# One linear-attention and GeGLU kernel: phi in another form on three engines, K weights on ScalarE's DMA queue, later weights behind the crossbar transposes

## The chip, the cores and the metric

The kernel runs on one core of a Trainium2 chip. The metric is the device time of one execution in microseconds (us), as the median of several runs.

## The reference

The input x has 2048 rows of 576 values in bf16. After a layer norm, two branches read the same normalised rows, and both results are added to x. Branch A is linear attention with 32 heads of 18 values; branch B is a gated feed-forward network (FFN) with 4608 hidden values. Cut to what matters:

```python
xn = _layernorm(x)
# branch A
qkv = (xn @ wqkv).reshape(B, S, 3, H, Dh)         # H = 32, Dh = 18
phi = lambda t: jnp.where(t > 0, t + 1, jnp.exp(t)) + 1e-6
pq, pk = phi(q), phi(k)
kv  = jnp.einsum("bhsd,bhse->bhde", pk, v)
z   = jnp.einsum("bhsd->bhd", pk)
num = jnp.einsum("bhqd,bhde->bhqe", pq, kv)
den = jnp.einsum("bhqd,bhd->bhq", pq, z)[..., None] + 1e-6
attn = (num / den) @ wo
# branch B
ffn = (gelu(xn @ w_gate) * (xn @ w_up)) @ w_down
out = x + attn + ffn
```

## The kernel before, in words

The 2048 rows are 16 tiles of 128 rows. Work falls into two large stages, and each engine executes its own instructions strictly in the order in which the program issues them.

**The attention stage.** For every tile n the kernel does these steps; the names are those of the code.

- `ln_stats` (L212, L213) on VectorE (DVE) takes mean and variance, `ln_rstd` (L217, L218) on ScalarE (ACT) takes the reciprocal root, `ln_norm` (L221) on DVE writes the normalised rows `xn`, and `ln_dup` (L227) copies the last 64 columns once more, on GpSimd (POOL) for the first four tiles and on DVE after that.
- `xn` is transposed into `xnT`. The first four tiles go through TensorE (PE), `transposes` (L236), and a copy out of PSUM, `tp_copy` (L239). The other twelve go through the DMA crossbar, `dma_transposes` (L242), issued from SyncE (SP).
- `k_half` (L250) computes K for one tile in two halves of 288 columns, into PSUM banks 5 and 6 (for tile 1 into banks 0 and 1).
- phi of K is made in three steps a half: `k_relu` (L270) and `k_exp` (L274) on ACT make exp(-relu(-t)) in the f32 tile `phi_e`, and `k_sum` (L278) on DVE adds max(t, 0) from PSUM and writes `pk`. The name `hT` in the profile at L278 is the storage that `pk` shares.
- `g_accumulate` (L294) adds pk of the tile, multiplied with `xn`, to the matrix G, from which the kv product and z are later made without ever forming V. `pk` has one more column of ones, from which the constant 1e-6 of phi is added when G is copied out (`g_copy`, L539 to L546).

The Q side works in 20 units (`q_unit`, L347), each a group of up to seven heads by 512 rows. phi of Q takes `q_relu` (L381) and `q_exp` (L385) on ACT, `q_eps` (L389) on POOL, which adds 1e-6, and `q_sum` (L393) on DVE. The first 14 units run singly; the last six run as three pairs (`q_pair`) whose two matmul streams use the two halves of the PE rows (L318).

The order of all this is written out by hand. The tables `STEPS` and `Q_STEPS` give each step a due time per tile, the last entry repeating every `TILE` = 2.94; the list `todo` is sorted by those times and issued in that order. Some small matmuls without use (`spin`, L138) keep PE busy early on. In `todo` also stand the loads of the V weights (`load_w(2, ...)`, L109 and L112) and of the first four FFN weight blocks (`load_gu`, L176 to L180), one step a tile from 18.0 on. They are issued by SP, between the crossbar transposes.

At the start SP issues all loads in one queue: x tiles 0, 1, 2 and 3, then the K weights, x tiles 4 to 7, the Q weights, and x tiles 8 to 15. ACT loads its function table (L132) meanwhile.

**The FFN stage.** For four groups of 512 rows, 18 blocks (`gu_pair`) each compute two chunks of gate and up values. A `_Unit` runs the gate and the up matmuls side by side on the two halves of the PE rows, in two passes `p1` and `p2`; between the passes the halves change banks, and a `nop` on another engine (the relay, L327) orders that turn. The relay engine is SP for blocks 0 and 1 and POOL for later ones. `load_gu` for a later block stands ahead of `p1` on SP from block 1 on, and waits until its buffers are free. Then ACT takes the gelu (L634), DVE multiplies (L635), and after 18 blocks the down projection (L664, L669) follows.

Of the kernel before, what the change touches and what calls it, by code (L numbers as in the profile page):

```python
# [8 lines left out]
ACT = mybir.ActivationFunctionType  # L9
ALU = mybir.AluOpType  # L10
# [5 lines left out]
P = 128  # L16
HP = 64
# [21 lines left out]
NWARM = 38  # L39
TD = 4  # L40
XW = 642
PKW = 578


class _Ring:
# [11 lines left out]
def kernel(  # L57
# [34 lines left out]
    def load_x(n0, cnt):  # L92
        nc.sync.dma_start(x_sb[:, n0:n0 + cnt, :], x_view[:, n0:n0 + cnt, :])  # L93
# [10 lines left out]

    wq_lo = apool.tile([P, D], BF16, name="wq_lo")

    def load_w(which, k0=0, k1=4):
        c = slice(which * D, (which + 1) * D)
        nc.sync.dma_start(  # L109
            wqkv_sb[:, k0:k1, c], A_wqkv[k0 * P:k1 * P, c].rearrange("(kt p) c -> p kt c", p=P))  # L110
        if k1 == 4:
            nc.sync.dma_start(wqkv_sb[0:HP, 4, c], A_wqkv[512:576, c])  # L112
            if which == 0:
                nc.sync.dma_start(wq_lo[HP:P, :], A_wqkv[512:576, c])

# [11 lines left out]
    make_identity(nc, ident[:])  # L127
    eps_ln = const.tile([P, 1], F32, name="eps_ln")
    nc.vector.memset(eps_ln[:], EPS_LN)
    eps_att = const.tile([P, 1], F32, name="eps_att")  # L130
    nc.vector.memset(eps_att[:], EPS_ATT)
    nc.scalar.preload_act_table_set("natural_log_exp_and_others")  # L132
    nc.vector.memset(wqkv_sb[HP:P, 4, :], 0.0)

    def spin(count):
# [47 lines left out]

    xn = apool.tile([P, NS, XW], BF16, name="xn")
    nc.gpsimd.memset(xn[:, :, 640:641], 1.0)
    nc.gpsimd.memset(pk[:, :, D:D + 1], 1.0)

    bmask = const.tile([P, CR], F32, name="bmask")
    bm3 = bmask[:].rearrange("p (h e) -> p h e", e=DH)
# [75 lines left out]
        hs = slice(hf * HALF, (hf + 1) * HALF)  # L265
        return ps_all[:, k_bank(n, hf), :HALF], k_e[n][:, hs], pk[:, n, hs]

    def k_relu(n, hf):
        ps, e, _ = k_part(n, hf)
        nc.scalar.activation(out=e, in_=ps, func=ACT.Relu, scale=-1.0)  # L270

    def k_exp(n, hf):
        _, e, _ = k_part(n, hf)
        nc.scalar.activation(out=e, in_=e, func=ACT.Exp, scale=-1.0)  # L274

    def k_sum(n, hf):
        ps, e, out_ = k_part(n, hf)
        nc.vector.scalar_tensor_tensor(out=out_, in0=ps, scalar=0.0, in1=e, op0=ALU.max, op1=ALU.add)  # L278

    G_A = {
        0: [(0, 0, 0, 288), (1, 0, 288, 289)],
        1: [(2, 0, 0, 288), (3, 0, 288, 289)],
        4: [(0, 288, 0, 224), (1, 289, 224, 223), (2, 288, 447, 130)],
    }
    G_B = {2: [(5, 0, 0, 288), (6, 0, 288, 289)], 3: [(0, 0, 0, 288), (1, 0, 288, 289)]}
    eps_sum = const.tile([P, KT], F32, name="eps_sum")

    def g_accumulate(n, pieces):  # L290
        for kt, ps_ in pieces.items():
# [80 lines left out]
    def q_at(i):  # L372
        sc, c = divmod(i, NCH)
        rows = DH * HCH[c]
        if i not in q_e:
            q_e[i] = phi_tile()[:rows, :SC]
        return q_e[i], q_out[i], pqT[:rows, c, sc * SC:(sc + 1) * SC]

    def q_relu(i):
        e, ps, _ = q_at(i)  # L380
        nc.scalar.activation(out=e, in_=ps, func=ACT.Relu, scale=-1.0)  # L381

    def q_exp(i):
        e, _, _ = q_at(i)
        nc.scalar.activation(out=e, in_=e, func=ACT.Exp, scale=-1.0)  # L385

    def q_eps(i):
        e, _, _ = q_at(i)
        nc.gpsimd.tensor_scalar(out=e, in0=e, scalar1=1.0, scalar2=EPS_ATT, op0=ALU.mult, op1=ALU.add)  # L389

    def q_sum(i):
        e, ps, out_ = q_at(i)
        nc.vector.scalar_tensor_tensor(out=out_, in0=ps, scalar=0.0, in1=e, op0=ALU.max, op1=ALU.add)  # L393

    def mask_pair(dst, b4, b1):

# [63 lines left out]
    def den_norm(sc, c, q, pieces):  # L460
# [14 lines left out]
    TILE = 2.94  # L475
    x_ = None
    STEPS = [
        (ln_stats, [3.05, 3.99, 6.43, 7.37, 8.65, 10.92, 14.71, 16.48]),
        (ln_rstd, [4.17, 5.11, 7.56, 8.55, 10.38, 13.51, 15.94, 18.79]),
        (ln_norm, [x_, 5.70, 8.31, 9.59, 11.86, 14.13, 17.42, 20.27]),  # L480
        (ln_dup, [5.61, 6.18, 8.79, 10.07, 12.34, 14.61, 17.90, 20.75]),
        (transposes, [x_, 6.58, 9.09, 10.37]),
        (tp_copy, [x_, 7.00, 9.54, 11.09]),
        (dma_transposes, [x_, x_, x_, x_, 12.58, 14.85, 18.14, 20.99]),
        (lambda n: k_half(n, 0), [6.87, 9.38, 10.66, 13.72, 16.57, 20.24, 22.61, 25.46]),
        (lambda n: k_half(n, 1), [7.48, 8.10, 11.27, 14.33, 17.18, 19.63, 22.00, 24.85]),
        (lambda n: k_relu(n, 0), [7.99, 10.81, 11.93, 14.46, 17.31, 21.11, 23.35, 26.20]),
        (lambda n: k_relu(n, 1), [8.27, 9.26, 12.67, 15.20, 18.05, 20.37, 22.78, 25.59]),
        (lambda n: k_exp(n, 0), [8.98, 12.95, 12.39, 14.92, 17.77, 21.57, 23.91, 26.76]),
        (lambda n: k_exp(n, 1), [10.10, 11.65, 13.23, 15.66, 18.51, 20.83, 23.63, 26.48]),  # L490
        (lambda n: k_sum(n, 0), [9.93, 13.41, 12.85, 15.65, 18.60, 22.03, 24.45, 27.30]),
        (lambda n: k_sum(n, 1), [10.56, 12.44, 13.77, 16.12, 18.97, 21.29, 24.09, 26.94]),
        (lambda n: g_accumulate(n, G_A), [12.97, 14.94, 15.82, 17.80, 23.22, 24.10, 26.08, 29.13]),
    ]

    Q_STEPS = [
        (q_unit, [11.89, 18.55, 20.85, 26.83, 29.88]),
        (q_relu, [13.94, 19.76, 22.28, 28.04, 31.09]),
        (q_exp, [16.37, 24.19, 27.04, 30.10, 33.16]),
        (q_eps, [17.05, 24.87, 27.72, 30.78, 33.84]),  # L500
        (q_sum, [18.00, 25.75, 28.60, 31.66, 34.72]),
    ]
    NQ = 12

# [6 lines left out]

    todo = [*timed(STEPS, NS), *timed(Q_STEPS, NQ)]

    for n, (na, nb, ta, tb, ca, cb) in enumerate([(4.93, 5.31, 5.31, 5.91, 5.62, 6.16)]):
        todo += [
            (na, lambda n: ln_norm(n, 0, 3 * P), n), (nb, lambda n: ln_norm(n, 3 * P, D), n),
            (ta, lambda n: transposes(n, 0, 3, 7), n), (tb, lambda n: transposes(n, 3, KT, 4), n),
            (ca, lambda n: tp_copy(n, 0, 3, 7, acopy), n), (cb, lambda n: tp_copy(n, 3, KT, 4, vcopy), n),
        ]

    todo += [(t, spin, count) for t, count in [(5.70, 4), (6.23, 3), (6.60, 5), (10.42, 2)]]

    loads = [lambda n, i=i: load_gu(i // 2, i % 2) for i in range(2 * NWBUF)]
    loads.insert(1, lambda n: load_w(2, 0, 2))
    loads.insert(3, lambda n: load_w(2, 2, 4))
    todo += [(18.0 + TILE * i, step, 0) for i, step in enumerate(loads)]
    todo.sort(key=lambda x: x[0])

    tail = next(i for i, (_, step, n) in enumerate(todo) if step is STEPS[-1][0] and n == NS - 1) + 1
# [2 lines left out]


    def g_copy(kt, pieces, on):

        m = P if kt < 4 else HP + 1
        eps = eps_sum[:m, kt:kt + 1]
        b, col, _, w = pieces[kt][-1]
        nc.vector.tensor_scalar_mul(out=eps, in0=ps_all[:m, b, col + w - 1:col + w], scalar1=EPS_ATT)  # L539
        for (b, col, d0, w), eng in zip(pieces[kt][::-1], on):  # L540
            w = min(w, D - d0)
            out_, in_ = g_sb[:m, kt, d0:d0 + w], ps_all[:m, b, col:col + w]
            if eng is nc.scalar:
                nc.scalar.activation(out=out_, in_=in_, func=ACT.Identity, bias=eps, scale=1.0)
            else:
                nc.vector.tensor_scalar_add(out=out_, in0=in_, scalar1=eps)  # L546

    for n in range(NS):
        g_accumulate(n, {2: G_B[2]})
    g_copy(4, G_A, (nc.vector, nc.scalar, nc.vector))  # L550
    g_copy(0, G_A, (nc.scalar, nc.vector))
    g_copy(1, G_A, (nc.scalar, nc.vector))
    for _, step, n in todo[tail:]:
        step(n)
    q_unit(12)
    for step in (q_relu, q_exp, q_eps, q_sum):
        step(12)
    for n in range(NS):
# [43 lines left out]
    def gu_pair(sc, k):  # L602
# [4 lines left out]
        for i in range(GUB):  # L607
            b = [banks.next(), banks.next()]
            fcol = slice(i * P, (i + 1) * P)

            def lhs(a, rows, kt, fcol=fcol):
                if kt == 4:
                    return wr[rows, fcol]
                return (wg, wu)[a][rows, kt, fcol]

            u = _Unit([ps_all[:, b[0], :], ps_all[:, b[1], :]], lhs, lambda a, rows, kt: xnT[rows, kt, cs],
                      nc.sync if blk < 2 else nc.gpsimd)
            if blk > 0:
                load_gu(blk + NWBUF - 1, i)
            u.p1()  # L620
            units.append((b, u))
# [106 lines left out]
```

## Time and profile before

| what | value |
|---|---|
| median of 3 runs | 525.21 us (524.9 to 526.15) |
| profiled execution | 526.45 us |
| its span, first to last instruction | 524.7 us |
| PE busy | 517.2 us (99%) |
| DVE busy | 248.4 us (47%) |
| ACT busy | 147.9 us (28%) |
| POOL busy | 40.1 us (8%) |
| mean granted TensorE clock | 1.000 |

The profile is one execution on the chip. PE is TensorE's matmuls, PEld its weight loads, SPq the issuing of SyncE. Times in it count from the span's start. A busy PE is not PE at its peak: matmuls are pipelined and their ends are modelled, so the durations of neighbours overlap. An engine's idle time is put down to what released it.

### The profile page before, as it was taken

Reading aid. Unit: us, or ns where it says so; the run is one execution under the profiler, and the core shown is the slowest. Engines: PE = TensorE matmul, PEld = TensorE weight load, DVE = VectorE, ACT = ScalarE, POOL = GpSimd, SP = SyncE. Lnnn points to the kernel's source line nnn. Section 1 sums busy time; section 2 is a strip of 40 time slices with the busy share of each in tenths; the row PEclk is TensorE's granted clock in tenths of the full one; section 3 lists DMA queues with packets and bytes.
Section 4 is the critical chain, followed back from the end, with each engine's and each line's share of the span. In section 5 each row is a group of like instructions: output and inputs, shape, how many; then the busy total and the mean of one; then the engine's idle time right before and its main releaser. Section 6 shows DMA issues by size and latency. Waiting matters only on the chain.

```text
span 524.7 us, 10664 instructions
## 1 busy us (share of the span) xinstructions
PE 517.2 (99%) x4502; PEld 315.8 (60%) x4502; DVE 248.4 (47%) x426; ACT 147.9 (28%) x301; POOL 40.1 (8%) x63
## 2 busy tenths in 40 slices
PE   7999999999999999999999999999999999999997
PEld 7767764555577754444577744444777544445775
DVE  7887545977348423333388134333584233333110
ACT  5989563233230012332200033232000123222000
POOL 2012130121001100000011000000011000000000
PEclk9999999999999999999999999999999999999999
DMA  8565009999500035555300065555100355540000
GB/s 262 135 156 119 1 2 240 264 268 265 169 21 24 12 103 158 158 144 158 108 12 13 28 174 143 156 159 151 32 22 12 104 158 157 144 130 1 12 11 24
DMA packets 106443, 57.90 MB, mean 110 GB/s; under 512 B 13402, under 2 KB 105754, under 8 KB 106394
## 3 DMA queue, kind: packets, MB, share of 16 engines
q1 hardware_dynamic: 106394, 57.21, 38.8%
q8 instruction: 35, 0.57, 0.4%
q14 instruction: 14, 0.11, 0.1%
HBM read 52.86 MB, written 2.36 MB: 105 GB/s over the span
## 4 chain that ended last, share of the span: by engine, by line
PE 96%; DMA 2%; ACT 1%; DVE 0%; SPq 0%; issue 0%; DVEq 0%
PE ps_all L318 55%; PE ps_all L664 27%; PE ps_all L669 4%; PE ps_all L294 3%; PE ps_all L250 3%; PE ps_all L347 3%; DMA wqkv_sb<-in_A_wqkv_dram 1%; DMA xnT<-xn 1%; PE ps_all L442 1%; PE ps_all L424 0%; PE ps_all L646 0%; SPq L93 0%; ACT phi_e L270 0%; DVE hT L278 0%; ACT xnT L239 0%; ACT phi_e L274 0%
## 5 line engine op out<-in xcount | busy, mean ns | idle before, releaser
L318 PE MATMUL ps_all<-xnT,wg 64*128 64x512 bf16 x1152 | 273.0, 376 | 0.0
L318 PE MATMUL ps_all<-xnT,wu 64*128 64x512 bf16 x1152 | 271.6, 376 | 0.0
L635 DVE TENSOR_TENSOR hT<-ps_all,gl 128x512 bf16<-128x512 f32 x144 | 99.4, 691 | 161.2 <-ACT gl L634 160.7
L634 ACT ACTIVATE gl<-ps_all 128x512 f32<-128x512 f32 x144 | 86.0, 598 | 312.7 <-PE ps_all L318 295.8
L318 PEld LDWEIGHTS <-wu 64*128 64x128 bf16 x1152 | 108.1, 94 | 66.0 <-SPq L327 0.7
L318 PEld LDWEIGHTS <-wg 64*128 64x128 bf16 x1152 | 108.1, 94 | 65.7 <-issue 0.5
L664 PE MATMUL ps_all<-wd_sb,hT 128*128 128x288 bf16 x1152 | 147.0, 286 | 0.0
L664 PEld LDWEIGHTS <-hT 128*128 128x128 bf16 x1152 | 112.3, 98 | 30.6 <-issue 1.3
L466 DVE RECIPROCAL den_sb<-den_sb 126x128 f32<-126x128 f32 (+1 forms) x80 | 68.3, 911 | 0.5
L672 DVE TENSOR_TENSOR res<-ps_all,x_sb 128x288 bf16<-128x288 f32 x32 | 14.6, 458 | 88.0 <-PE ps_all L669 88.0
L318 PE MATMUL ps_all<-xnT,wr 64*128 64x512 bf16 x288 | 55.7, 376 | 0.0
L469 POOL TENSOR_TENSOR pqT<-pqT,den_sb 126x512 bf16<-126x512 bf16 (+3 forms) x25 | 24.1, 965 | 299.2 <-DVE den_sb L466 276.0
L669 PE MATMUL ps_all<-m_sb,pqT 126*128 126x288 bf16 (+1 forms) x160 | 24.9, 285 | 0.0
L318 PEld LDWEIGHTS <-wr 64*128 64x128 bf16 x288 | 14.6, 94 | 16.7 <-issue 0.7
L250 PE MATMUL ps_all<-wqkv_sb,xnT 128*128 128x288 bf16 x160 | 22.5, 286 | 1.7 <-DMA wqkv_sb<-in_A_wqkv_dram 0.8
L294 PE MATMUL ps_all<-hT,xn 128*128 128x288 bf16 (+4 forms) x176 | 22.4, 276 | 0.0
L294 PEld LDWEIGHTS <-xn 128*128 128x128 bf16 (+1 forms) x176 | 17.5, 102 | 4.3
L250 PEld LDWEIGHTS <-xnT 128*128 128x128 bf16 x160 | 15.3, 98 | 7.6 <-issue 1.3
L393 DVE SCALAR_TENSOR_TENSOR pqT<-ps_all,phi_e 126x512 bf16<-126x512 f32 (+1 forms) x20 | 13.4, 672 | 12.4 <-POOL phi_e L389 12.4
L669 PEld LDWEIGHTS <-pqT 126*128 126x128 bf16 (+1 forms) x160 | 15.5, 97 | 4.1
L347 PE MATMUL ps_all<-xnT,wqkv_sb 128*126 128x512 bf16 (+1 forms) x70 | 17.4, 378 | 0.0
L389 POOL TENSOR_SCALAR phi_e<-phi_e 126x512 f32<-126x512 f32 (+1 forms) x20 | 12.4, 618 | 54.2 <-DVE hT L278 29.8
(63 smaller groups left out, 183.8 us busy)
## 6 DMA issues: line engine op xcount, KB each, us to landing
wg<-in_B_w_gate_dram SPq DMA_DIRECT2D x72, 256.0 KB, 2.9
wu<-in_B_w_up_dram SPq DMA_DIRECT2D x72, 256.0 KB, 3.5
wd_sb<-in_B_w_down_dram SPq DMA_DIRECT2D x12, 432.0 KB, 4.7
wr<-in_B_w_gate_dram SPq DMA_DIRECT2D x72, 32.0 KB, 2.7
wr<-in_B_w_up_dram SPq DMA_DIRECT2D x72, 32.0 KB, 3.1
out_dram<-res SPq DMA_DIRECT2D x15, 144.0 KB, 1.8
wqkv_sb<-in_A_wqkv_dram SPq DMA_DIRECT2D x2, 576.0 KB, 6.0
x_sb<-in_A_x_dram SPq DMA_DIRECT2D x2, 576.0 KB, 7.2
```

Source lines behind the costliest of these rows:

```text
L250: nc.tensor.matmul(ps_all[:, k_bank(n, hf), :HALF], lhsT=xnT[:, kt, n * P:(n + 1) * P], rhs=wqkv_sb[:, kt, D + hf * HALF:D + (hf + 1) * HALF],
L294: nc.tensor.matmul(ps_all[:m, b, col:col + w], lhsT=xn[:, n, j0:j0 + m], rhs=pk[:, n, d0:d0 + w], start=(n == 0 and col == 0), stop=(n == ...
L318: return nc.tensor.matmul(self.outs[i], lhsT=self.lhs(i, rows, kt), rhs=self.rhs(i, rows, kt), start=start, stop=stop, skip_group_check=True,)
L347: nc.tensor.matmul(ps, lhsT=wqkv_sb[:, kt, q0:q0 + rows], rhs=xnT[:, kt, sc * SC:(sc + 1) * SC], start=(kt == 0), stop=(kt == KT - 1),)
L393: nc.vector.scalar_tensor_tensor(out=out_, in0=ps, scalar=0.0, in1=e, op0=ALU.max, op1=ALU.add)
L466: nc.vector.reciprocal(out=d[:, h:h + P], in_=d[:, h:h + P])
L469: nc.gpsimd.tensor_tensor(out=pqT[:rows, c, cols], in0=pqT[:rows, c, cols], in1=d, op=ALU.mult)
L634: nc.scalar.activation(out=gl[:], in_=ps_all[:, b[0], :], func=ACT.Gelu_apprx_tanh)
L635: nc.vector.tensor_tensor(out=hT[:, GUB * k + i, :], in0=ps_all[:, b[1], :], in1=gl[:], op=ALU.mult)
L664: nc.tensor.matmul(acc, lhsT=hT[:, f, j * P:(j + 1) * P], rhs=wd_sb[:, f, hs], start=(f == 0), stop=False,)
L669: nc.tensor.matmul(acc, lhsT=pqT[:rows, c, ts_], rhs=m_sb[:rows, c, hs], start=False, stop=(c == NCH - 1),)
L672: nc.vector.tensor_tensor(out=res[:, hs], in0=acc, in1=x_sb[:, n, hs], op=ALU.add)
```

## The change

- **phi.** phi(t) is written as max(t + 1 + 1e-6, min(exp t, 1) + 1e-6). `phi_exp` on ACT takes exp straight from PSUM, `phi_min` on POOL takes the minimum with 1 and adds 1e-6, `phi_max` on DVE adds 1 + 1e-6 to the PSUM value and takes the maximum. K and Q use the same three steps. The column of ones in `pk` goes, and `g_copy` becomes plain copies.
- **K weights.** Their two loads are issued from ACT's queue, after the table load, which moves to the front. x tiles 4 to 7 become one load on SP, right after tiles 2 and 3.
- **Later weights.** The V weights and the first four FFN blocks are issued by SP after the last step of `todo[:tail]`, so after the last crossbar transpose.
- **Order.** `STEPS` and `Q_STEPS` have new due times, there are ten spins where there were fourteen, and the relay of FFN block 1 is POOL.

```diff
-PKW = 578
+PKW = 576
...
+    nc.scalar.preload_act_table_set("natural_log_exp_and_others")
+    load_w(1, nc.scalar)
     load_x(0, 1)
     load_x(1, 1)
     load_x(2, 2)
-    load_w(1)
-    load_x(4, 2)
-    load_x(6, 2)
+    load_x(4, 4)
     load_w(0)
...
-    nc.scalar.preload_act_table_set("natural_log_exp_and_others")
...
-    def k_relu(n, hf):
-        ps, e, _ = k_part(n, hf)
-        nc.scalar.activation(out=e, in_=ps, func=ACT.Relu, scale=-1.0)
...
+    def phi_exp(ps, e, out_):
+        nc.scalar.activation(out=e, in_=ps, func=ACT.Exp)
+
+    def phi_min(ps, e, out_):
+        nc.gpsimd.tensor_scalar(out=e, in0=e, scalar1=1.0, scalar2=EPS_ATT, op0=ALU.min, op1=ALU.add)
+
+    def phi_max(ps, e, out_):
+        nc.vector.scalar_tensor_tensor(out=out_, in0=ps, scalar=1.0 + EPS_ATT, in1=e, op0=ALU.add, op1=ALU.max)
...
-        (ln_stats, [3.05, 3.99, 6.43, 7.37, 8.65, 10.92, 14.71, 16.48]),
+        (ln_stats, [3.10, 4.04, 5.52, 7.57, 8.51, 11.53, 14.13, 16.64]),
...
-        (ln_norm, [x_, 5.70, 8.31, 9.59, 11.86, 14.13, 17.42, 20.27]),
-        (ln_dup, [5.61, 6.18, 8.79, 10.07, 12.34, 14.61, 17.90, 20.75]),
+        (ln_norm, [x_, 6.73, 7.23, 9.83, 10.53, 13.55, 16.39, 18.90]),
+        (ln_dup, [5.66, 7.21, 7.71, 10.31, 11.01, 14.03, 16.87, 19.38]),
...
-        (dma_transposes, [x_, x_, x_, x_, 12.58, 14.85, 18.14, 20.99]),
-        (lambda n: k_half(n, 0), [6.87, 9.38, 10.66, 13.72, 16.57, 20.24, 22.61, 25.46]),
-        (lambda n: k_half(n, 1), [7.48, 8.10, 11.27, 14.33, 17.18, 19.63, 22.00, 24.85]),
+        (dma_transposes, [x_, x_, x_, x_, 11.25, 14.27, 17.11, 19.62]),
+        (lambda n: k_half(n, 0), [7.80, 9.58, 10.20, 13.53, 16.36, 18.66, 21.71, 24.64]),
+        (lambda n: k_half(n, 1), [6.88, 8.97, 11.10, 14.14, 16.97, 19.28, 22.32, 25.25]),
...
+        (lambda n: phi_exp(*k_part(n, 0)), [8.54, 10.52, 10.94, 14.27, 17.10, 19.40, 22.45, 25.38]),
...
+        (lambda n: phi_min(*k_part(n, 0)), [9.00, 11.11, 11.52, 14.99, 17.56, 20.12, 22.91, 25.84]),
+        (lambda n: phi_min(*k_part(n, 1)), [8.08, 10.70, 12.30, 15.40, 18.17, 20.53, 23.52, 26.45]),
+        (lambda n: phi_max(*k_part(n, 0)), [9.47, 12.47, 12.83, 15.67, 18.03, 21.12, 23.96, 26.36]),
+        (lambda n: phi_max(*k_part(n, 1)), [10.17, 11.17, 13.19, 16.03, 18.64, 21.48, 24.32, 26.92]),
...
-    loads = [lambda n, i=i: load_gu(i // 2, i % 2) for i in range(2 * NWBUF)]
-    loads.insert(1, lambda n: load_w(2, 0, 2))
-    loads.insert(3, lambda n: load_w(2, 2, 4))
-    todo += [(18.0 + TILE * i, step, 0) for i, step in enumerate(loads)]
+    todo += [(t, spin, count) for t, count in [(5.70, 3), (6.10, 5), (8.30, 2)]]
...
+    load_w(2)
+    for i in range(NWBUF):
+        load_gu(i, 0)
+        load_gu(i, 1)
     for n in range(NS):
         g_accumulate(n, {2: G_B[2]})
...
-                      nc.sync if blk < 2 else nc.gpsimd)
+                      nc.sync if blk == 0 else nc.gpsimd)
```

## The prediction, written before the changed kernel was run

> **What bounds the kernel now.** I read the page's engine table first (PE 99% busy), then the chain of work that ended last, then the same chain, the windows and the timelines of the first 82 us, because the diff touches nothing after the second FFN block. The page's chain, by engine:
>
> ```profile
> PE 96%; DMA 2%; ACT 1%; DVE 0%; SPq 0%; issue 0%; DVEq 0%
> ```
>
> So only the 4% that is not PE, about 20 us, can be won, and most of that lies before PE's first matmul or in waits early on. Windows (busy us of PE, PEld, DVE, ACT, POOL, then granted clock, DMA share, GB/s):
>
> ```profile
> 0.00:8.24 8.24, 5.99 (x61) 5.88 (x61) 5.82 (x20) 3.73 (x8) 3.09 (x16) 1.00 0.76 218
> 8.24:30.41 22.17, 20.63 (x162) 15.60 (x161) 19.25 (x59) 19.79 (x59) 2.33 (x5) 1.00 0.68 185
> 30.41:55.00 24.59, 24.59 (x178) 18.14 (x179) 18.42 (x49) 21.58 (x57) 4.38 (x8) 1.00 0.52 119
> 81.61:524.70 443.09, 439.40 (x3870) 258.05 (x3866) 191.78 (x274) 87.70 (x151) 24.13 (x25) 1.00 0.38 110
> ```
>
> From 30.41 on PE has no gap, though ACT is 88% and DVE 75% busy there: taking work from ACT buys nothing in that stage. The chain in order of time (start, length, what) shows what holds PE before it:
>
> ```profile
> 2.20 6.00 DMA wqkv_sb<-in_A_wqkv_dram
> 8.24 1.40 PE ps_all L250 x10
> ...
> 11.12 0.59 ACT xnT L239
> ...
> 15.33 0.83 DVE hT L278 x2
> ...
> 25.84 4.52 DMA xnT<-xn
> ```
>
> PE's own timeline, where it stood idle (bracket at the end):
>
> ```profile
> 11.75 0.44 PE L236 MATMUL ps_all<-ident,xn 128*128 128x128 bf16 x5 [0.62 <-ACT xnT L239]
> 16.20 0.77 PE L250 MATMUL ps_all<-wqkv_sb,xnT 128*128 128x288 bf16 x5 [0.21 <-DVE hT L278]
> 30.41 1.40 PE L250 MATMUL ps_all<-wqkv_sb,xnT 128*128 128x288 bf16 x10 [0.70 <-DMA xnT<-xn]
> ```
>
> The first K matmul waits for the K weights, issued at 2.20 and landed at 8.20. The brackets understate the holes, since a matmul's modelled end overlaps the next. By the chain's steady prices (10 K matmuls 1.23, 7 G 0.75, 5 Q 1.08) the holes are 0.76 (10.99 to 11.75), 0.38 (15.82 to 16.20) and 0.87 (29.54 to 30.41): **2.0 us**. As a check, 8.24 to 67.53 is 59.3 us and holds 160 K matmuls (19.6), 16 x 7 and 64 of G (20.0), 14 Q units (15.1), the z and kv stages (1.7) and 0.8 of transposes and spins, 57.2 in all: 2.1 are holes. A last hole is in FFN block 1, by the waits from 67 to 90 us:
>
> ```profile
> PEld L318 <- SPq L327: 0.7, 2, 0.5
> ```
>
> Block 0 takes 3.88 us (73.41 to 77.29), block 1 4.32 (to 81.61): 0.44 lost, mostly because its turn nops sit on SP behind load_gu(4), which waits for block 0 to free its weights.
>
> **What the skill says.** The Trainium skill, "DMA: Bandwidth & Descriptors", "Issuing engines are not separate DMA queues": DMAs of SP, ScalarE and GpSimd run on the same 16 DMA engines, and a second issuer only saves issue time; "Queues, rings and completion order" adds that an engine takes turns between queues packet by packet. The trace has one data queue (q1), so no run here shows two. "ScalarE: Activation LUTs", "What ACT_TABLE_LOAD costs": 1283 ns for the load; the trace agrees (1283 at 0.80). It prices a 288-wide ACTIVATE at 186 + 0.833 x 288 = 426 ns; the trace has 408 and 437. "SBUF — State Buffer", "Who interferes with whom": a DVE copy or tensor_scalar in a two-port mode and any GpSimd instruction exclude one another for the whole instruction. ln_norm (0.42 us) and the ln_dup copy (0.18) are of that kind, the PSUM-reading sums are not. In the trace L389 always takes 0.62 and falls beside no ln_norm, so nothing shows it.
>
> **The change part by part.**
>
> *ScalarE.* Per K half one 0.41 us relu goes (32, 13.1 us), per Q unit one of 0.59 (20, 11.7 us). After 30.41 this lies beside full PE: zero, covered by PE's queue of matmuls. Before, it frees the ACT queue behind which the xnT copy stood (11.12): that hole, 0.76, should go, and with it the late exps behind the 0.38 one.
>
> *GpSimd.* 32 new minimums of 128x288 f32. Price: between these rows (count, busy us, mean ns),
>
> ```profile
> L389 POOL TENSOR_SCALAR phi_e<-phi_e 126x512 f32<-126x512 f32 (+1 forms) x20 | 12.4, 618 | 54.2 <-DVE hT L278 29.8 <-ACT phi_e L385 20.8 <-DVE g_sb L546 3.4
> L227 POOL COPY xn<-xn 128x64 bf16<-128x64 bf16 x4 | 0.9, 237 | 6.7 <-DVE xn L221 6.7
> ```
>
> a line through 64 and 512 elements gives 0.43 us at 288; bounds 0.24 and 0.62. POOL then works 2 x 0.43 + 0.62 = 1.48 of each 3.05 us tile: no bound. The chain of a K half was relu 0.41 + exp 0.44 + sum 0.45 = 1.30 and becomes exp 0.41 + min 0.43 + max 0.45 = 1.29, and its exp no longer queues behind the other half's relu. It must end before the next tile's matmul reuses bank 5 or 6, 2.44 us after its own. Cost zero, if DVE stays on time. DVE in one steady tile:
>
> ```profile
> 39.46 0.81 DVE L212 BATCH_NORM_STATS2 stats<-x_sb 128x6 f32<-128x288 bf16 x2
> ...
> 40.43 0.64 DVE L393 SCALAR_TENSOR_TENSOR pqT<-ps_all,phi_e 126x512 bf16<-126x512 f32 x1
> 40.98 0.42 DVE L221 TENSOR_SCALAR xn<-x_sb,mv,rstd 128x576 bf16<-128x576 bf16 x1
> 41.44 0.18 DVE L227 COPY xn<-xn 128x64 bf16<-128x64 bf16 x1
> ...
> 41.77 0.82 DVE L278 SCALAR_TENSOR_TENSOR hT<-ps_all,phi_e 128x288 bf16<-128x288 f32 x2
> ```
>
> It repeats at 42.51, so 3.05 us hold about 2.9 of work: 0.15 spare. The new order is stats, q max, both k max, ln_norm, ln_dup; the minimums come before the k max, so POOL should be idle when ln_norm runs. In the first tiles the two can collide; I allow 0.4 us (two ln_norms behind a 0.43 minimum, half of it reaching PE); bounds 0 and 1.5.
>
> *K weights on ScalarE's queue.* Issue moves from 2.20 to between 0.85 (if the trigger doesn't wait for the table load) and 2.1 (if it does). But the K weights were 1224 KB deep in one queue (576 KB of x ahead of 648), and now share with x and the Q weights, all issued sooner. By equal bytes they end after 2 x 648 = 1296 KB, as before. By turns of rows, x 4 to 7 (rows of 4608 bytes against 1152) also go first: 576 KB more, 1.8 us at about 330 GB/s (5 to 10 us moved 333). The best case is 1.2 us: x's side is no sooner, since DVE's copy of tile 0, ended at 6.95, now has stats(2) (0.94) ahead of it instead of ln_norm(1) (0.4), with stats(2) waiting for x 2 and 3 (landed at 5.4 before, later when shared). I take **+0.2**, from -1.2 to +1.8. The two issues also stand on ACT ahead of rstd(0), which is not needed before 4.15: zero.
>
> *Later weights behind the transposes.* SP held 19 loads between the transposes; they now follow the last one (ended 49.28). At about 0.55 us an issue SP ends near 60, and 2.95 MB at 150 to 300 GB/s land by 59 to 69, V weights first (about 55; L424 needs them at 66), FFN block 0 before 60 (needed at 73.4). SP's relays for the Q pairs come at 67.5, after that. Cost zero, cover some 10 us. The transpose landing 4.52 us after issue, against a median of 2.9, loses its company, and ln_norm(8) comes earlier in the order: the 0.87 hole goes.
>
> *Relay of block 1 on GpSimd.* POOL's last minimum ends before 77.9 and the nop is due at about 79.4: **-0.4** (bounds -0.45 and 0); SP's load waits hold nobody.
>
> *The rest.* Five eps_sum steps (0.15 each) leave DVE under full PE; 80 matmul columns of 0.43 ns, four spins in idle time, two small memsets: zero.
>
> Sum: start +0.2, ramp -2.0 + 0.4, block 1 -0.4 = **-1.8**. The profiled execution took 526.45 (span 524.7 and 1.75 around it), which would be 524.6; it stood 1.24 over the median of 525.21, so the forecast is **523.4**.
>
> **The rivals.**
> 1. *K weights late.* The queues take turns by row: PE starts near 10 instead of 8.24 (+1.8), the ramp gains 1.4, block 1 0.4: 525.2. For it: the 4608-byte rows and the sooner Q weights; against it: the saved issue time.
> 2. *The port lock, slower.* In each steady tile a 0.43 us minimum stands in front of ln_norm, and DVE needs 2.9 + 0.43 = 3.33 us where PE needs 3.05. It decides from 0.15 us of added wait a tile; then k max frees banks 5 and 6 late and PE waits 0.28 in each of 12 tiles: +3.4. With the start +0.2, the ramp -0.9 and block 1 -0.4 that is +2.3: 527.5. For it: DVE's thin slack; against it: the new order and the minimums ahead of k max.
> 3. *The two-queue start saves time.* The trigger passes the table load and fills gaps in the DMA stream (61 to 138 GB/s near 3.5 us in the DMA view): start -1.2, 522.0. That the queue doesn't help at all is inside the main case.
>
> **How the numbers follow.** Main case 0.40 (522.6 to 524.4), rival 1 0.27, rival 2 0.18, rival 3 0.10, else 0.05. A measurement can tell about 0.3%, 1.6 us, from no change: below 523.6 is faster, above 526.8 slower. Main case: two thirds of it gains over 1.6, so faster 0.26; rival 3 0.10; a little of rival 1 and the rest 0.04. Rival 2 gives 0.16 slower, rival 1 and the rest 0.04. So faster 0.40, same 0.40, slower 0.20. The range 521.6 to 527.2 takes rival 3 at its bound and most of rival 2.
>
> **What would show it.** Right: first K matmul at 8 to 9 us, no PE wait for an xnT copy or a transpose DMA after it, transposes landing near 2.9, no SPq L327 wait in block 1, POOL near 26 us for 52 minimums. Wrong: K weights landing past 10, PE waiting for the k max every tile, or ln_norm well over 0.42 us.

## The result, and the profile after

The changed kernel takes **554.15 us** (median of 4 runs, 553.4 to 554.41) against 525.09 for the kernel before on the same chip (4 runs): a ratio of 1.0547, 95% interval 1.0528 to 1.0565, or 29 us slower. The forecast was 523.4 us, with a range that ended at 527.2: the sign was wrong and the time is far outside. The profiled execution has a span of 552.7 us against 524.7, so 28.0 us of it can be located in the trace.

From the page of the changed kernel: its engine table, two rows of the 40 slices (each 13.8 us, busy tenths), and the chain that ended last by engine.

```profile
PE 524.5 (95%) x4498; PEld 311.5 (56%) x4498; DVE 249.7 (45%) x420; ACT 127.8 (23%) x249; POOL 103.8 (19%) x94
...
PE   6787789799999999999999999999999999999997
...
POOL 4899965501100120000001200000011000000000
...
PE 84%; POOL 9%; DVE 3%; issue 2%; DMA 1%; ACT 0%; SPq 0%; POOLq 0%; ACTq 0%
```

POOL holds 19% of the span on average, which looks harmless; the slices show that this is 90% and more in slices 3 to 5 and 50 to 90% in slices 2 and 6 to 8, the stretch in which PE's row falls mostly to 7 and 8. The chain confirms it: POOL, absent from the chain of before, carries 9% of the span, some 50 us. One line does it. This is the answer about `phi_e` over the first 110 us (min/median/max in ns, first and last start, shapes):

```profile
L266 POOL TENSOR_SCALAR phi_e<-phi_e x52: 1171/1172/1920, 10.5 to 102.2; 128x288 f32<-128x288 f32 x32, 126x512 f32<-126x512 f32 x16, 72x512 f32<-72x512 f32 x4
```

The prediction had 0.43 us for the 288-column minimum and 0.62 for the 512-column one; they take **1.17 and 1.92**. POOL's timeline shows the consequence:

```profile
24.63 11.51 POOL L266 TENSOR_SCALAR phi_e<-phi_e 128x288 f32<-128x288 f32 x8 [0.60 <-ACT phi_e L263]
36.79 40.49 POOL L266 TENSOR_SCALAR phi_e<-phi_e 128x288 f32<-128x288 f32 x27 [0.66 <-ACT phi_e L263]
82.38 1.92 POOL L266 TENSOR_SCALAR phi_e<-phi_e 126x512 f32<-126x512 f32 x1 [5.10 <-ACT phi_e L263]
```

The middle row is 27 minimums back to back in 40.49 us. With about 1.25 us from one 288-column step to the next and 2.0 for a 512-column one that is 18 and 9, nine tiles of 4.5 us each, where PE needs 3.05 us a tile. PE follows POOL, as its timeline in one of these tiles shows (bracket: idle before, and what ended it):

```profile
43.09 0.77 PE L244 MATMUL ps_all<-wqkv_sb,xnT 128*128 128x288 bf16 x5 [0.71 <-DVE hT L269]
44.34 0.77 PE L244 MATMUL ps_all<-wqkv_sb,xnT 128*128 128x288 bf16 x5 [0.48 <-DVE hT L269]
```

The second K half starts 1.25 us after the first, which is POOL's step and not PE's own 0.62: each half waits for the k max (`hT`, L269) that frees its PSUM bank, and that waits for a minimum. The waits of the first 120 us (total us, times, longest) say it as a chain, PE behind DVE behind POOL:

```profile
DVE pqT L269 <- POOL phi_e L266: 20.9, 11, 5.9
DVE hT L269 <- POOL phi_e L266: 20.5, 28, 1.9
...
PE ps_all L244 <- DVE hT L269: 14.3, 24, 1.0
...
PE ps_all L308 <- DVE pqT L269: 4.8, 4, 1.6
```

In windows (PE, PEld, DVE, ACT, POOL busy; granted clock, DMA share, GB/s) the stretches are these:

```profile
8.56:88.30 79.74, 63.01 (x457) 44.77 (x457) 45.97 (x121) 31.22 (x82) 64.35 (x49) 0.98 0.34 83
88.30:104.90 16.60, 11.84 (x101) 5.88 (x102) 5.69 (x10) 5.61 (x9) 12.50 (x7) 0.95 0.18 45
104.90:124.00 19.10, 19.09 (x154) 8.87 (x155) 10.11 (x16) 4.78 (x8) 0.67 (x1) 0.86 0.63 178
```

POOL is busy 64.35 of the first 79.74 us, PE only 63.01. The 28.0 us divide as follows. The first K matmul starts at 8.56 instead of 8.24: +0.3. From there to FFN block 0 it takes 85.54 us (to 94.10) instead of 65.17: **+20.4**, nearly all of it in the stretch where POOL is full. Some 1.3 us of it is no POOL wait: from 8.56 to 11.36 PE is busy throughout, at a granted clock of 0.53 (2.8 x 0.47), after 2.21 us of idle time; e5 and e7 below come back to that. The remaining +7.3 lies in the first FFN blocks: the last six Q units reach POOL within about 3 us (their exps start no later than 94.9), its 512-column minimums run from 92.23 at 2 us apiece to 104.1, and PE's first FFN matmuls wait four times for a q max (L308 on `pqT`, 4.8 us). After those waits the granted clock of the third window is 0.86, worth 19.1 x 0.14 = 2.7 us more.

### The profile page after: what moved, and what is told of

The parts are those of the page before. It is cut to its first block, busy times and chain, and to the rows that moved or that the text cites. A ratio compares the mean times of both kernels' runs of the same rounds, so it can differ in the third digit from the quotient of the medians.

```text
span 552.7 us, 10654 instructions
## 1 busy us (share of the span) xinstructions
PE 524.5 (95%) x4498; PEld 311.5 (56%) x4498; DVE 249.7 (45%) x420; ACT 127.8 (23%) x249; POOL 103.8 (19%) x94
## 4 chain that ended last, share of the span: by engine, by line
PE 84%; POOL 9%; DVE 3%; issue 2%; DMA 1%; ACT 0%; SPq 0%; POOLq 0%; ACTq 0%
PE ps_all L308 51%; PE ps_all L630 26%; POOL phi_e L266 9%; PE ps_all L635 4%; PE ps_all L284 2%; DVE stats L206 1%; DVE xn L215 1%; DMA x_sb<-in_A_x_dram 1%; PE ps_all L420 1%; PE ps_all L244 0%; PE ps_all L337 0%; DVE mv L207 0%; DVE xn L221 0%; PE ps_all L402 0%; DVE pqT L269 0%
## 5 line engine op out<-in xcount | busy, mean ns | idle before, releaser
L308 PE MATMUL ps_all<-xnT,wg 64*128 64x512 bf16 x1152 | 275.1, 378 | 0.0
L308 PE MATMUL ps_all<-xnT,wu 64*128 64x512 bf16 x1152 | 270.6, 379 | 0.0
L308 PEld LDWEIGHTS <-wg 64*128 64x128 bf16 x1152 | 108.6, 94 | 74.1 <-issue 7.1
L308 PEld LDWEIGHTS <-wu 64*128 64x128 bf16 x1152 | 107.4, 94 | 68.0 <-issue 0.9
L266 POOL TENSOR_SCALAR phi_e<-phi_e 128x288 f32<-128x288 f32 (+2 forms) x52 | 76.1, 1464 | 17.1 <-ACT phi_e L263 13.4
L308 PE MATMUL ps_all<-xnT,wr 64*128 64x512 bf16 x288 | 62.9, 377 | 4.8 <-DVE pqT L269 4.8
L244 PE MATMUL ps_all<-wqkv_sb,xnT 128*128 128x288 bf16 x160 | 25.6, 293 | 14.3 <-DVE hT L269 14.3
L263 ACT ACTIVATE phi_e<-ps_all 128x288 f32<-128x288 f32 (+2 forms) x52 | 24.5, 481 | 42.8 <-PE ps_all L244 24.5
L308 PEld LDWEIGHTS <-wr 64*128 64x128 bf16 x288 | 17.2, 94 | 18.5 <-issue 2.2
L284 PE MATMUL ps_all<-hT,xn 128*128 128x288 bf16 (+2 forms) x176 | 22.4, 275 | 2.4 <-DVE hT L269 2.4
L269 DVE SCALAR_TENSOR_TENSOR hT<-ps_all,phi_e 128x288 bf16<-128x288 f32 x32 | 14.5, 454 | 20.5 <-POOL phi_e L266 20.5
L269 DVE SCALAR_TENSOR_TENSOR pqT<-ps_all,phi_e 126x512 bf16<-126x512 f32 (+1 forms) x20 | 13.8, 690 | 20.9 <-POOL phi_e L266 20.9
```

The lines of the kernel that those rows point to most:

```text
L244: nc.tensor.matmul(ps_all[:, k_bank(n, hf), :HALF], lhsT=xnT[:, kt, n * P:(n + 1) * P], rhs=wqkv_sb[:, kt, D + hf * HALF:D + (hf + 1) * HALF],
L263: nc.scalar.activation(out=e, in_=ps, func=ACT.Exp)
L269: nc.vector.scalar_tensor_tensor(out=out_, in0=ps, scalar=1.0 + EPS_ATT, in1=e, op0=ALU.add, op1=ALU.max)
L284: nc.tensor.matmul(ps_all[:m, b, col:col + w], lhsT=xn[:, n, j0:j0 + m], rhs=pk[:, n, d0:d0 + w], start=(n == 0 and col == 0), stop=(n == ...
L308: return nc.tensor.matmul(self.outs[i], lhsT=self.lhs(i, rows, kt), rhs=self.rhs(i, rows, kt), start=start, stop=stop, skip_group_check=True,)
```

## The experiments

The theory after the result, A: GpSimd's minimum-and-add is itself a slow instruction, whatever stands around it. Its rival B: the instruction is lengthened or placed badly by its company (DVE's exclusion, the new order), and a cheap one in its place would be slow too. A third, C, puts the loss on the moved loads and the new order. On the rest of the change, theory D: a second DMA queue at the start costs time instead of saving it; its rival E: it saves time.

**e1_mult: the changed kernel with the minimum made a multiplication by 1** (phi then lacks the minimum).

```diff
-        nc.gpsimd.tensor_scalar(out=e, in0=e, scalar1=1.0, scalar2=EPS_ATT, op0=ALU.min, op1=ALU.add)
+        nc.gpsimd.tensor_scalar(out=e, in0=e, scalar1=1.0, scalar2=EPS_ATT, op0=ALU.mult, op1=ALU.add)
```

> The changed kernel with the minimum in phi_min replaced by a multiplication with 1 (the minimum is left out of phi; everything else, the instruction count included, stays). Theory A, the minimum itself is dear on GpSimd (1.17 us at 288 elements where the multiply-add was 0.62 at 512) and GpSimd is the bound at 4.5 us a tile: the 52 steps take about 0.43 and 0.62 us, GpSimd's busy sum for them falls from 76 to about 26 us, and the time falls to 522 to 527. Rival B, the step is long because VectorE's two-port instructions lock GpSimd out: the multiplication meets the same lock, stays near 1.2 us, and the time stays above 545. Rival C, the moved loads and the new order cost the time: steps short, time still above 540.

Measured: 525.46 us, ratio 1.0003 (0.9991 to 1.0015). Same shapes, same places, same neighbours, one operator different, in the answer about `phi_e`:

```profile
L266 POOL TENSOR_SCALAR phi_e<-phi_e x52: 431/432/634, 10.8 to 76.6; 128x288 f32<-128x288 f32 x32, 126x512 f32<-126x512 f32 x16, 72x512 f32<-72x512 f32 x4
```

0.43 and 0.63 us are, to 0.01, the forecast's two prices, and with them 28.7 of the 29 us are gone. From 8 us to FFN block 0 PE has no wait for a k max at all. A stands, B falls, and so does C.

**e2_price: a price list.** In the kernel before, spare `tensor_scalar` steps on a scratch tile of 128x288 f32, four of each kind, issued in the FFN stage where POOL is idle.

```diff
+        if j == 0:
+            g(**ts(pr[:], pr[:], ALU.min, ALU.add))
+        if j == 1:
+            g(**ts(pr[:], pr[:], ALU.mult, ALU.add))
...
+        if j == 3:
+            g(**ts(pr[:], pr[:], ALU.min, ALU.max))
...
+            if sc in (1, 2):
+                price(k // 2)
```

> The kernel before, with one more GpSimd tensor_scalar on a scratch tile after each FFN block of the second and third row groups (nothing of the output depends on them), nine kinds, four of each: min+add, mult+add, add+min, min+max, max+add, a lone min, add+mult in f32 at 128x288; min+add in bf16 at 288; min+add in f32 at 64. Theory A: every kind with a min or max takes about 1.17 us at 288, mult+add and add+mult about 0.43; at 64 the min+add about 0.42 (0.21 fixed and 3.35 ns an element, the line through 1.17 at 288 and 1.92 at 512). Rival B (the lock): in this stage VectorE does little in two-port modes, so min+add takes 0.43 too.

Measured, groups of instructions kept apart by form (busy us, mean ns): L592 is min+add, L594 mult+add, L598 min+max, L608 min+add on 64 columns.

```profile
L592 POOL TENSOR_SCALAR pr<-pr 128x288 f32<-128x288 f32 x4 | 4.7, 1173 | 29.9 <-PE ps_all L318 29.9
...
L594 POOL TENSOR_SCALAR pr<-pr 128x288 f32<-128x288 f32 x4 | 1.7, 432 | 12.3 <-PE ps_all L318 12.3
...
L598 POOL TENSOR_SCALAR pr<-pr 128x288 f32<-128x288 f32 x4 | 1.7, 426 | 12.3 <-PE ps_all L318 12.3
L608 POOL TENSOR_SCALAR pr<-pr 128x64 f32<-128x64 f32 x4 | 1.7, 425 | 13.8 <-PE ps_all L318 13.8
```

Alone in an idle stage min+add takes the same 1.17 us as in the busy one, so nothing around it lengthens it. The others: add+min 1177 ns, max+add 1177, add+mult 430, min+add on bf16 1174, a lone minimum 930. Two expectations missed: min+max, expected dear, is cheap at 426, and the lone minimum lies between, at 930 instead of 1170. The 64-column row gives the slope: (1.17 - 0.425) / 224 = 3.3 ns a column, against (0.634 - 0.432) / 224 = 0.9 for mult+add.

**e3_phi: the kernel before with the new phi alone** (min+add on POOL, one exp on ACT, the rest untouched).

```diff
-        nc.scalar.activation(out=e, in_=ps, func=ACT.Relu, scale=-1.0)
+        nc.scalar.activation(out=e, in_=ps, func=ACT.Exp)
...
-        nc.scalar.activation(out=e, in_=e, func=ACT.Exp, scale=-1.0)
+        nc.gpsimd.tensor_scalar(out=e, in0=e, scalar1=1.0, scalar2=0.0, op0=ALU.min, op1=ALU.add)
...
-        nc.vector.scalar_tensor_tensor(out=out_, in0=ps, scalar=0.0, in1=e, op0=ALU.max, op1=ALU.add)
+        nc.vector.scalar_tensor_tensor(out=out_, in0=ps, scalar=1.0, in1=e, op0=ALU.add, op1=ALU.max)
```

> The kernel before with the new form of phi alone (exp on ScalarE, minimum on GpSimd, maximum on VectorE), each step in the place of an old one in the order; loads, relays and due times as before. Theory A: nearly the whole loss is here, 545 to 556 us, with GpSimd back to back from about 12 to 75 us. Rival C (loads and order): 523 to 530.

Measured: 551.03 us, ratio 1.0489 (1.0456 to 1.0522), nearly the whole loss. PE's timeline has the same picture in the old order, one tile every 4.47 us:

```profile
34.28 1.24 PE L347 MATMUL ps_all<-xnT,wqkv_sb 128*126 128x512 bf16 x5 [0.71 <-DVE pqT L392]
...
36.52 0.77 PE L250 MATMUL ps_all<-wqkv_sb,xnT 128*128 128x288 bf16 x5 [0.36 <-DVE hT L278]
...
38.75 1.24 PE L347 MATMUL ps_all<-xnT,wqkv_sb 128*72 128x512 bf16 x5 [0.71 <-DVE pqT L392]
```

**e4_rest: the changed kernel with the old phi arithmetic** (relu and exp on ACT, a mult+add of epsilon on POOL for K and Q).

```diff
-        nc.scalar.activation(out=e, in_=ps, func=ACT.Exp)
+        nc.scalar.activation(out=e, in_=ps, func=ACT.Relu, scale=-1.0)
+        nc.scalar.activation(out=e, in_=e, func=ACT.Exp, scale=-1.0)
...
-        nc.gpsimd.tensor_scalar(out=e, in0=e, scalar1=1.0, scalar2=EPS_ATT, op0=ALU.min, op1=ALU.add)
+        nc.gpsimd.tensor_scalar(out=e, in0=e, scalar1=1.0, scalar2=EPS_ATT, op0=ALU.mult, op1=ALU.add)
...
-        nc.vector.scalar_tensor_tensor(out=out_, in0=ps, scalar=1.0 + EPS_ATT, in1=e, op0=ALU.add, op1=ALU.max)
+        nc.vector.scalar_tensor_tensor(out=out_, in0=ps, scalar=0.0, in1=e, op0=ALU.max, op1=ALU.add)
```

> The changed kernel with the old arithmetic of phi (relu and exp on ScalarE, multiply by 1 and add 1e-6 on GpSimd for K and Q alike, maximum with 0 and sum on VectorE): loads, order and relay are those of the changed kernel. Theory A, with my first reading of the rest: 522 to 527. ScalarE has its old load again, so the hole at the xnT copy may stay (up to +0.8 against the version with one ScalarE pass). Rival C: above 540.

Measured: 530.29 us, ratio 1.0101 (1.008 to 1.0123), a miss: 3 us over the top of what was expected. The run isn't a clean "rest of the change". ACT's timeline (start, length) shows Q relus 3.11 us apart with nothing idle between, against PE's 3.05:

```profile
22.98 0.58 ACT L263 ACTIVATE phi_e<-ps_all 126x512 f32<-126x512 f32 x1
...
26.09 0.58 ACT L263 ACTIVATE phi_e<-ps_all 126x512 f32<-126x512 f32 x1
```

The new order is laid out for one ScalarE pass; two passes fill the engine and put a POOL step into the chain besides, and PE waits for k max and q max again. How much each of these makes up was not separated.

**e5_minmax: the changed kernel with a cheap operator pair.** The epsilon becomes a floor instead of an addend, so that the second operator is a maximum.

```diff
-        nc.gpsimd.tensor_scalar(out=e, in0=e, scalar1=1.0, scalar2=EPS_ATT, op0=ALU.min, op1=ALU.add)
+        nc.gpsimd.tensor_scalar(out=e, in0=e, scalar1=1.0, scalar2=EPS_ATT, op0=ALU.min, op1=ALU.max)
...
-        nc.vector.scalar_tensor_tensor(out=out_, in0=ps, scalar=1.0 + EPS_ATT, in1=e, op0=ALU.add, op1=ALU.max)
+        nc.vector.scalar_tensor_tensor(out=out_, in0=ps, scalar=1.0, in1=e, op0=ALU.add, op1=ALU.max)
```

> The changed kernel with one operator of phi_min exchanged: minimum with 1, then maximum with 1e-6, in place of minimum with 1, then add 1e-6 (phi then has 1e-6 as a floor under the exponential, not as an addend; the minimum stays). In the price run min+max took 0.43 us at 288, min+add 1.17. Theory A (the pair min+add is the dear thing, not the minimum): GpSimd steps at 0.43 and 0.62, time 524 to 527 like the multiplication run, 27 us under the changed kernel. Rival A2 (any GpSimd minimum is dear inside the attention stage): above 545.

Measured: 524.35 us, ratio 0.9992 (0.9982 to 1.0001). The same minimum is taken, by the same engine, in the same 52 places, and the kernel is 30 us under the changed one. In its trace PE has no hole between 8.58 us and FFN block 0. What that execution lost of the forecast gain it lost at the start, in PE's timeline:

```profile
1.43 4.07 PE L133 MATMUL ps_all<-ident 128*128 128x128 bf16 x38 [1.43 <-POOL ident masks.py:199]
7.61 0.34 PE L230 MATMUL ps_all<-ident,xn 128*128 128x128 bf16 x3 [2.10 <-DVE xn L215]
...
8.58 1.36 PE L244 MATMUL ps_all<-wqkv_sb,xnT 128*128 128x288 bf16 x5
```

PE stands for 2.10 us, and the five K matmuls after that take 1.36 us instead of 0.77: up to 448 ns each, where 286 is the median.

**e6_onequeue: e5 with the loads at the start as before.** The K weights go back to SP's queue behind x 0 to 3; the later weights stay behind the transposes.

```diff
-    load_w(1, nc.scalar)
...
-    load_x(4, 4)
+    load_w(1)
+    load_x(4, 2)
+    load_x(6, 2)
```

> The run e5_minmax with the loads at the start as in the kernel before: K weights on SP behind x tiles 0 to 3, x tiles 4 to 7 as two loads. Theory D, the second queue takes DMA turns from x, so that x tile 1 lands at 6.1 instead of 4.0, PE stands idle from 5.7 to 7.5 and its next matmuls run slowly (447 ns instead of 286): without it the K matmuls start near 8.2 at 286 ns, and the time falls by 1 to 2.5 us against e5_minmax, to 522 to 524. Rival E, the second queue brings the K weights sooner and that is worth more: slower than e5_minmax.

Measured: **523.62 us, ratio 0.9974 (0.9967 to 0.9982)**, the fastest of all and faster than the kernel before. PE's timeline; the second row is the only wait that it names after the first K matmul and before FFN block 0:

```profile
8.17 0.77 PE L245 MATMUL ps_all<-wqkv_sb,xnT 128*128 128x288 bf16 x5 [1.12 <-DMA wqkv_sb<-in_A_wqkv_dram]
...
26.10 1.39 PE L245 MATMUL ps_all<-wqkv_sb,xnT 128*128 128x288 bf16 x10 [0.17 <-DVE hT L270]
```

From the first K matmul to FFN block 0 it is 63.7 us (8.17 to 71.87), 1.5 less than before. Against e5 the second queue costs 0.7 us in the medians, less than the 1 to 2.5 expected; the two intervals just touch.

**e7_warm: e5 with more spins**, which keep PE busy until tile 0 arrives.

```diff
-NWARM = 38
+NWARM = 58
```

> The run e5_minmax with 58 spins at the start instead of 38, so that PE has work until about 7.7 us. Theory D2, of the loss at the start most is the slow matmuls after PE's idle time (10 K matmuls at 1.20 a five instead of 0.62, transposes at 0.53 instead of 0.28: about 2 us): K matmuls at 286 ns from the first, start 0 to 0.3 later, time 1 to 2 us under e5_minmax. If they stay slow, the idle time isn't their cause: same as e5_minmax.

Measured: 524.19 us, ratio 0.9985 (0.9978 to 0.9992). The profile shows full-speed matmuls now:

```profile
1.43 6.04 PE L133 MATMUL ps_all<-ident 128*128 128x128 bf16 x58 [1.43 <-POOL ident masks.py:199]
...
8.34 0.81 PE L244 MATMUL ps_all<-wqkv_sb,xnT 128*128 128x288 bf16 x5
```

FFN block 0 starts at 72.35 instead of 73.71, yet the medians differ by 0.16 only, where 1 to 2 were expected. The single executions show why. Of e5's 13, five have a mean granted clock of 0.996 or 0.997 and take 525.15 to 525.62 us; the profiled one is among them. The other eight have 0.999 or 1.000 and take 523.96 to 524.94. The two medians lie 1.4 us apart. All 18 of e7 have 0.999 or 1.000 and take 523.93 to 524.70. So by clock and time the idle PE is slowed in some executions and not in others, where it is slowed it costs about 1.4 us, and with PE kept busy none of the 18 shows it. e5's median falls among the eight and hides it.

**e8_relay: the kernel before with only block 1's relay moved to GpSimd.**

```diff
-                      nc.sync if blk < 2 else nc.gpsimd)
+                      nc.sync if blk == 0 else nc.gpsimd)
```

> The kernel before with one edit: the relay of FFN block 1 on GpSimd. By my prediction's step, block 1 shrinks from 4.32 to 3.9 us and the SPq L327 wait is gone: 0.4 us less, 524.6; within what the measurement can tell. Rival: GpSimd's last q_eps (to 77.9) holds the relay and nothing changes.

Measured: 524.71 us, ratio 0.9995 (0.9987 to 1.0003). In PE's timeline block 1 takes 3.94 us (76.12 to 80.06) instead of 4.32, and no wait for SP is left; in the time 0.4 us can't be told from nothing. Nor is the 4.32 a constant: with the relay on SP as before, block 1 takes 3.89 us in e12, 3.94 in e2, 4.04 in e10, 4.37 in e9 and 4.50 in e11. SP's own timeline tells why. This is one weight load of block 1's time in the kernel before:

```profile
78.08 1.35 SPq L177 DMA_DIRECT2D wr<-in_B_w_gate_dram  x1
```

and the same load in e12:

```profile
77.90 0.50 SPq L177 DMA_DIRECT2D wr<-in_B_w_gate_dram  x1
```

The relay nops wait behind a load whose issue takes sometimes 0.5 and sometimes 1.35 us; on GpSimd they don't. Between these traces the move is worth nothing to 0.6 us of block 1.

**e9_later: the kernel before with only the later loads moved behind the last transpose.**

```diff
-    loads = [lambda n, i=i: load_gu(i // 2, i % 2) for i in range(2 * NWBUF)]
...
+    load_w(2)
+    for i in range(NWBUF):
+        load_gu(i, 0)
+        load_gu(i, 1)
```

> The kernel before with one edit: V weights and the first four FFN blocks issued after the last crossbar transpose. By my prediction's step the transpose of tile 8 lands 2.6 to 3 us after its issue instead of 4.52 and the 0.87 us hole before tile 8's K matmuls goes: up to 0.9 less, 524.1 to 525; nothing waits for the later weights. Rival: the hole stays because ln_norm(8) is late on VectorE, no change.

Measured: 525.32 us, ratio 1.0005 (0.9997 to 1.0013). The hole that was to go is still there, in PE's timeline:

```profile
29.37 1.40 PE L250 MATMUL ps_all<-wqkv_sb,xnT 128*128 128x288 bf16 x10 [0.67 <-DVE stats L212]
```

The transpose in front of it again landed 4.5 us after its issue at 24.84, though no weights were moving; the later ones took 2.6. At 29.3 us that landing and the end of a DVE stats step coincide, as they do before (30.36 and 30.32), so which of them releases PE is not settled. That the loads were the cause is refuted.

**e10_price2: more pairs**, in the same way as e2.

```diff
+        if j == 0:
+            g(**ts(pr[:], pr[:], ALU.min, ALU.min))
...
+        if j == 2:
+            nc.gpsimd.tensor_scalar_mul(out=pr[:], in0=pr[:], scalar1=1.0)
...
+        if j == 7:
+            g(**ts(pr[:], pr[:], ALU.subtract, ALU.mult))
+        if j == 8:
+            nc.vector.tensor_scalar(**ts(pr[:], pr[:], ALU.min, ALU.add))
```

> The kernel before with a second list of spare instructions on a scratch tile in the second and third row groups (the output doesn't depend on them): GpSimd tensor_scalar min+min, max+min, a lone mult, mult+min, a lone max, a lone add, min+max in bf16, subtract+mult, and VectorE min+add. If a pair is dear only where one operator is a min or max and the other an arithmetic one: min+min, max+min, bf16 min+max, subtract+mult at 0.43 us, mult+min at 1.17, lone mult and add at 0.43 or, if a lone operator is dear of itself, 0.93 like the lone minimum. VectorE's min+add takes under 0.4 us whatever the operators.

Measured (columns as above): L592 min+min, L596 a lone multiplication, L606 subtract+mult, L608 the dear min+add on DVE.

```profile
L592 POOL TENSOR_SCALAR pr<-pr 128x288 f32<-128x288 f32 x4 | 4.7, 1173 | 29.9 <-PE ps_all L318 29.9
...
L596 POOL TENSOR_SCALAR pr<-pr 128x288 f32<-128x288 f32 x4 | 3.7, 934 | 11.3 <-PE ps_all L318 11.3
...
L606 POOL TENSOR_SCALAR pr<-pr 128x288 f32<-128x288 f32 x4 | 4.7, 1181 | 12.3 <-PE ps_all L318 12.3
...
L608 DVE TENSOR_SCALAR pr<-pr 128x288 f32<-128x288 f32 x4 | 1.2, 300 | 0.0
```

The rule I expected, that only pairs of unlike operators are dear, is wrong: min+min costs as much as min+add. max+min took 1170 ns, mult+min 1174, a lone maximum 928, a lone addition 933; min+max on bf16 426. Of all pairs tried in e2 and e10, three are cheap: mult+add, add+mult and min+max.

**e11_kqueue: the kernel before with only the K weights on ScalarE's queue** (and x 4 to 7 in one load, ACT's table loaded first).

```diff
+    nc.scalar.preload_act_table_set("natural_log_exp_and_others")
+    load_w(1, on=nc.scalar)
...
-    load_w(1)
-    load_x(4, 2)
-    load_x(6, 2)
+    load_x(4, 4)
```

> The kernel before with the loads at the start alone as in the changed kernel: K weights on ScalarE's queue, x tiles 4 to 7 in one load. Theory D: K weights land near 5.4 instead of 8.2, but x tile 1 near 6 instead of 4, PE idles and then works at half rate for some matmuls: 0 to 2 us slower, 525 to 527. Rival E: faster by up to 1 us.

Measured: 527.5 us, ratio 1.0041 (1.0022 to 1.006), 2.2 us slower, a little over the 0 to 2 expected. DVE's timeline has the second tile's rows at 6.09, where before its stats ran at 4.04 without waiting:

```profile
6.09 0.82 DVE L211 BATCH_NORM_STATS2 stats<-x_sb 128x6 f32<-128x288 bf16 x2 [1.31 <-DMA x_sb<-in_A_x_dram]
```

Behind it on DVE stands ln_norm(0), so the transposes of tile 0 start at 7.46 instead of 5.45 and PE waits 2.24 us for them, as in e5. E falls and D stands for the new start as a whole: no run gave the K weights their own queue while x 4 to 7 stayed two loads, or put them ahead of x in one queue.

**e12_phi_minmax: the kernel before with the new phi alone, as min+max.** It is e3 with the second operator exchanged:

```diff
-        nc.scalar.activation(out=e, in_=e, func=ACT.Exp, scale=-1.0)
+        nc.gpsimd.tensor_scalar(out=e, in0=e, scalar1=1.0, scalar2=0.0, op0=ALU.min, op1=ALU.max)
```

> The kernel before with the new phi alone, as in the run e3_phi, but with minimum and maximum in phi_min in place of minimum and addition (1e-6 is then a floor under Q's exponential, not an addend). Theory A: the 25 us of e3_phi vanish by this one operator, 523.5 to 526; with one ScalarE pass the 0.76 and 0.38 us holes of the ramp should shrink. Rival A2: stays above 540.

Measured: 525.9 us, ratio 1.0011 (1.0004 to 1.0017). e3's 26 us are gone, so the pair decides in the old order too. But PE's holes stay (0.29, 0.21, 0.72 and 0.36 us): one ScalarE pass fewer wins nothing by itself.

## Why the prediction was wrong

**GpSimd: the step that failed.** The prediction priced the minimum by "a line through 64 and 512 elements", from a 64-column copy and the 512-column mult+add, and bounded it at 0.24 and 0.62. Both rows were right as rows; the hidden assumption was that a `tensor_scalar` costs by its size whatever its two operators are. e1, e2 and e5 show that it doesn't: 0.43 us as mult+add or min+max, 1.17 as min+add. The 512-column Q step, which I took over unchanged at 0.62 because it stood in the trace, had its first operator changed as well, to 1.92. So "POOL works 1.48 of each 3.05 us tile: no bound" should have read 4.5 of 3.05. The excess of 1.45 us in nine full tiles is 13 of the 20 us; most of the rest lies in the tiles around them, and about 1.3 in the half-speed start. My bounds covered the size of the instruction and not its kind, which is why the range missed as well. No rival had a term for it.

**The port lock (rival 2 and the allowance of 0.4).** Not the cause: in e1 and e5 the POOL steps stand in the same places and PE waits for no k max. The prediction says that before the change no POOL step falls beside an ln_norm; one does (18.93 to 19.55 us beside ln_norm's 19.27 to 19.70), and both keep their usual 0.62 and 0.43. In the changed kernel nine ln_norms run wholly inside a 512-column minimum. This one, in DVE's timeline, lies inside POOL's step from 43.88 to 45.80:

```profile
44.21 0.44 DVE L215 TENSOR_SCALAR xn<-x_sb,mv,rstd 128x576 bf16<-128x576 bf16 x1
```

The nine take 0.44 to 0.50 us against 0.42, and the minimums their usual 1.92, so the exclusion for a whole instruction that the prediction cites does not show there (which mode ln_norm runs in, no run shows). In e5 and e1 a single ln_norm (25.01 and 25.75) begins with a cheap POOL step of 0.6 us and takes 0.77: that is what exclusion would look like, and PE does not wait for it. The allowance should have been zero. The rival named the right sign and the right waiting line, k max freeing banks 5 and 6 late, for the wrong reason.

**K weights on ScalarE's queue.** The +0.2 for the first K matmul came close (8.24 to 8.56) by luck, for a reason I hadn't got. The weights did not keep their time: issued at 0.84, while the table load ran (0.80 to 2.08), they landed at about 5.4 instead of 8.2, as rival 3 hoped. They got there ahead of x, whose second tile came about 2 us later, and DVE's order put that wait in front of tile 0. I looked for the price in the weights' own arrival, and it was in what they displaced. The half-speed matmuls after PE's 2.1 us of idle time were in no case of mine. By itself this part costs 2.2 us (e11, interval 1.2 to 3.2), around my bound of +1.8.

**Later weights.** No PE or weight-load wait for V or FFN weights appears, in e5 and e6 neither, so "cost zero" held. "Loses its company" did not (e9). The hole does go where the new order meets the cheap phi (e5: none, e6: 0.17).

**Relay of block 1.** The mechanism was right, and with the relay on GpSimd block 1 takes 3.88 to 3.94 us in e1, e5, e6, e7 and e8 (4.57 in e4, where PE waits there for a q max). The -0.4 itself was read from one execution and is what that one lost: without the move the block takes 3.89 to 4.50.

**ScalarE.** "Zero after 30.41" fits e12, which has one pass fewer and is no faster. The early holes were put down to relus queued ahead of a copy; e12 takes these relus away and keeps four holes, of which 0.29 is still the wait for the xnT copy. Only the new order together with one pass closes them.

**The sum.** With the pair exchanged the change as a whole gives -0.4 us by its ratio (e5, interval -0.9 to +0.1), and -1.4 (-1.7 to -0.9) without the second queue (e6). So the forecast of -1.8 was 1.4 too hopeful even apart from GpSimd, and by the same ratios 1.0 of that is the new start of the loads; min+add instead of a cheap pair is the other 29.8 us (554.15 - 524.35).

## What to carry to other kernels

A duration read from a profile is the price of that instruction with its operators, not of its engine and size: before work is moved onto GpSimd, put the exact operator pair into an idle stage a few times and read it, and if it is dear look for another pair that serves (here a floor in place of an addend), since here one operator decided 30 us. Then divide the engine's work per tile by the bounding engine's time per tile, because a mean share of 19% can hide an engine that is full for 60 us. A load that is moved to a queue of its own arrives sooner at the cost of the loads beside it, so ask first which of them is needed first.

## What the runs showed of the hardware

- GpSimd's `tensor_scalar` on 128x288 depends on its ordered operator pair: 0.43 us for mult+add, add+mult and min+max; 1.17 to 1.18 for min+add, add+min, max+add, mult+min, min+min, max+min and subtract+mult; 0.93 for a single minimum, maximum, addition or multiplication, which is thus dearer than the cheap pairs. bf16 changes nothing (min+max 426, min+add 1174 ns). DVE takes 0.30 for min+add. Why these pairs differ no run shows.
- A trigger on ScalarE's queue does not wait for a running table load: issued at 0.84, the load ran from 0.80 to 2.08.
- About 2.1 us of idle time soon after the start could lead to K matmuls of 448 instead of 286 ns: a granted clock of 0.51 from 8.70 to 12.10 us in e5's trace, and a lower mean clock in five of its 13 executions. The Trainium skill, "TensorE: Matmul & The Clock Gate", "What's actually happening", describes a clock that falls to half when TensorE has been idle for a window of about 3.4 us; the traces agree in kind (e5 with half-speed matmuls, e7 with its spins without), at a shorter gap. After the Q waits of the changed kernel the granted clock was 0.50 from 106 to 109 us, 0.80 to 112, and full again after that.
- The first K matmul in the order of loads of before started at 8.24, 7.80 (e12), 7.63 (e8) and 7.25 us (e9): a single profile does not settle half a microsecond at the start.
